# Strassen's algorithm for the first channel product of batches 4 to 7, and a new order for the second half

## The chip, the core and the metric

The kernel runs on one NeuronCore of a Trainium2 chip. Its engines work side by side, each through its own queue in order: TensorE (PE, with weight loads shown as PEld), VectorE (DVE), ScalarE (ACT), GpSimd (POOL) and SyncE (SP, which here only issues DMAs). They wait for each other by semaphores. Matmuls write to one of eight PSUM banks, and VectorE or ScalarE reads them from there. The metric is the device time of one execution in microseconds, the median of the runs.

## The reference, cut to what matters

Two layers on 8 batches of 576 tokens: an attention with random features (8 heads of 64), and a mixer over tokens and then over channels.

```python
proj = einsum('bhsd,md->bhsm', x, omega); h = proj - sum(x*x)/2
phi  = exp(h - max(h)) / sqrt(m)                   # for q and k
num  = q_p @ (k_p^T v);  den = q_p . sum(k_p);  x = num / den
h  = relu(x^T @ w_tok1) @ w_tok2;  u = x + h^T      # tokens: 576 -> 256 -> 576
h2 = relu(u @ w_ch1) @ w_ch2                        # channels: 512 -> 1536 -> 512
out = u + h2
```

The two channel products are the largest part: per batch of 512 tokens, 512 x 1536 and 1536 x 512. Inputs and output are f32; the kernel multiplies in f16 and sums in f32.

## The kernel before

A batch has 576 tokens: 512 are worked on per batch, and the 64 left of each of the eight batches are collected into one more chunk of 512, the tail chunk, whose channel mix comes last. The stages of a batch are `attention` (L521), `token_mix` (L764), and `channel_mix` (L957).

`attention`: for each pair of heads, products with omega (L656, L668), exponentials on ScalarE (L514), a maximum over features on VectorE (`km`, L680) and its reciprocal (L682), the scaling of v by it on GpSimd (`vs`, L295), the sum over tokens (L701, L708), its copy `kvsb` (L286), the numerator (L734, L736), a reciprocal (L743) and the normalisation into x (L744, or L756 on ScalarE).

`token_mix`: two products (L777, L790), a relu between, and the residual sum u on VectorE (L793). A DMA transposes u to uT (L798). `token_tail` does the same for the 64 tokens left, of two batches at a time.

`channel_mix`, first product: 12 blocks of 128 channels, each of 4 matmuls with 512 columns (L966) into a bank of its own, and a relu out of the bank on ScalarE (L290) or VectorE (L292) into `r3`. Second product (`channel_out_fast`, from batch 1 on): Strassen's algorithm in Winograd's form on halves, 7 products of 12 matmuls with 256 columns (L916) in three banks X, Y and Z, with sums S of `r3` on VectorE (L295) ahead, sums T of the weights made once (L448), and reads out of the banks into `o` (L905). Then the stores (L952, and L945 for the tail chunk).

Nothing of the order is left to a scheduler. Each step is a job with a number. The list ORDER gives the order in which all jobs are issued, and so the order in each engine's queue; SLOT gives the buffer or bank that each job takes; MOVED names the engine of jobs that don't run on their usual one. The jobs' costs and keys aren't used any more when it runs. Loads are issued from GpSimd's and SyncE's queues, stores from ScalarE's and SyncE's.

Of the kernel before, what the change touches and what calls it, by code (L numbers as in the profile page):

```python
# [9 lines left out]
FP32 = mybir.dt.float32  # L10
# [158 lines left out]
def kernel(  # L169
# [687 lines left out]
    def channel_out_fast(c, key, jr):  # L857
# [38 lines left out]
        def bank_of(b, j0):  # L896
            return (b, c, j0) if tail else (b, c)
# [173 lines left out]
```

## Time and profile before

| | |
|---|---|
| runs | 276.75, 277.55, 277.63 us; median 277.55 |
| profiled execution, first to last instruction | 275.9 us (no device time of its own is given; 1.65 us under the median) |
| granted TensorE clock | 0.996 |
| PE busy | 266.6 us, 97%, 2503 matmuls |
| DVE busy | 222.9 us, 81% |
| ACT busy | 138.1 us, 50% |
| POOL busy | 91.2 us, 33% |
| moved by DMA | 39.66 MB, mean 144 GB/s |

How to read it: busy times count an instruction from its start to its end, and overlapping instructions of one engine once. The chain of waits follows the work back from the last instruction, at each step to what released it. A group's row gives count, busy time, mean of one in ns, and the idle time of the engine in front of such instructions with what ended it.

### The profile page before, as it was taken

The page shows a single profiled execution, that of the slowest core. Times are in us where ns is not written, and L with a number is a line of the kernel's source. Part 1 is how long each engine was busy: PE and PEld are TensorE (multiplying, and loading weights), DVE is VectorE, ACT ScalarE, POOL GpSimd, SP SyncE. Part 2 cuts the span into 40 slices and gives each one's busy share as a digit, 9 for nine tenths or more (in the row PEclk, how much of TensorE's full clock was granted, in tenths as well). Part 3 has the DMA queues.
Part 4 walks back from the last instruction along what each step waited for, and adds up shares of the span by engine and source line. Part 5 has one row for each costly group of instructions (what it writes and reads, how often), then busy time and mean ns, then how long its engine had stood idle before and what let it go on. Part 6 is the DMA issues. An engine that isn't in the chain of part 4 may idle for free.

```text
span 275.9 us, 6228 instructions
## 1 busy us (share of the span) xinstructions
PE 266.6 (97%) x2503; PEld 165.5 (60%) x2503; DVE 222.9 (81%) x462; ACT 138.1 (50%) x289; POOL 91.2 (33%) x115
## 2 busy tenths in 40 slices
PE   8789999999999999999999999999999999999993
PEld 3367455444567655755676656755676477446782
DVE  3897889876998799987999899978985992675992
ACT  3999941188685338734756456636654500040200
POOL 8994492063703490075019510600043000000001
PEclk9999999999999999999999999999999999999998
DMA  7999999999998999979989994840252304021125
GB/s 195 192 209 212 190 212 177 202 193 146 203 191 133 229 176 186 151 148 171 198 184 183 232 125 123 191 90 2 97 79 77 96 0 95 2 99 53 78 83 146
DMA packets 81292, 39.66 MB, mean 144 GB/s; under 512 B 63984, under 2 KB 77040, under 8 KB 81072
## 3 DMA queue, kind: packets, MB, share of 16 engines
q0 software_dynamic: 31744, 17.74, 44.2%
q1 hardware_dynamic: 47072, 15.50, 28.7%
q10 hardware_dynamic: 2448, 6.03, 5.6%
q8 instruction: 19, 0.31, 0.5%
q14 instruction: 9, 0.07, 0.1%
HBM read 35.95 MB, written 16.52 MB: 190 GB/s over the span
## 4 chain that ended last, share of the span: by engine, by line
PE 89%; DMA 6%; POOL 3%; DVE 0%; issue 0%; POOLq 0%
PE bank L966 33%; PE bank L916 25%; PE bank L777 5%; PE bank L790 5%; DMA w1m<-in_moe_w_tok_dram 4%; PE bank L1000 4%; PE bank L734 3%; PE bank L656 3%; PE bank L668 2%; PE bank L701 2%; DMA uT<-u 2%; POOL r L319 1%; PE bank L844 1%; PE bank L816 1%; PE bank L828 1%; PE bank L736 1%
## 5 line engine op out<-in xcount | busy, mean ns | idle before, releaser
L966 PE MATMUL bank<-uT,wc 128*128 128x512 f16 x376 | 90.4, 379 | 0.3 <-DMA uT<-u 0.3
L290 ACT ACTIVATE r<-bank 128x512 f16<-128x512 f32 (+1 forms) x84 | 46.9, 597 | 77.1 <-PE bank L966 62.0
L295 POOL TENSOR_TENSOR vs<-v,vs 128x512 f16<-128x512 f16 x31 | 33.2, 1074 | 91.2 <-DVE vs L682 60.5
L966 PEld LDWEIGHTS <-wc 128*128 128x128 f16 x424 | 38.3, 98 | 37.9 <-issue 1.1
L916 PEld LDWEIGHTS <-r 128*128 128x128 f16 x384 | 36.9, 98 | 8.1 <-issue 1.2
L514 ACT ACTIVATE kp<-bank 128x512 f16<-128x512 f32 x64 | 35.6, 622 | 10.4 <-PE bank L656 10.4
L514 ACT ACTIVATE qp<-bank 128x512 f16<-128x512 f32 x64 | 36.3, 616 | 8.9 <-PE bank L668 6.0
L680 DVE TENSOR_REDUCE km<-kp 128x8 f16<-128x1024 f16 x32 | 38.6, 1206 | 2.5 <-ACT kp L514 2.4
L292 DVE TENSOR_SCALAR r<-bank 128x512 f16<-128x512 f32 (+1 forms) x42 | 27.7, 672 | 12.0 <-PE bank L966 11.2
L744 DVE TENSOR_TENSOR x<-bank,rc 128x320 f16<-128x320 f32 x62 | 30.5, 492 | 2.1
L916 PEld LDWEIGHTS <-S 128*128 128x128 f16 x288 | 27.9, 98 | 5.4 <-issue 0.3
L905 DVE TENSOR_TENSOR o<-u,bank 128x512 f32<-128x512 f16 x28 | 19.0, 679 | 6.9 <-PE bank L916 6.8
L916 PE MATMUL bank<-T,r 128*128 128x256 f16 x192 | 23.8, 273 | 0.0
L916 PE MATMUL bank<-T,S 128*128 128x256 f16 x192 | 23.6, 273 | 0.0
L916 PE MATMUL bank<-wc,r 128*128 128x256 f16 x192 | 23.6, 273 | 0.0
L945 POOL DMA_DIRECT2D out_dram<-o x2 | 1.3, 648 | 60.9 <-issue 60.9
L793 DVE TENSOR_TENSOR u<-x,bank 128x512 f16<-128x512 f16 x28 | 17.8, 681 | 1.1 <-PE bank L790 1.0
L905 DVE TENSOR_TENSOR o<-o,bank 128x512 f32<-128x512 f32 (+1 forms) x27 | 16.6, 618 | 2.2 <-PE bank L916 1.6
L734 PEld LDWEIGHTS <-qp 128*128 128x128 f16 x256 | 13.8, 98 | 7.0 <-DVE kvsb L286 0.2
L734 PE MATMUL bank<-kvsb,qp 128*128 128x65 f16 x256 | 15.6, 193 | 0.0
L743 DVE RECIPROCAL rc<-bank 128x5 f32<-128x5 f32 x62 | 11.5, 186 | 4.1 <-PE bank L736 2.7
L701 PEld LDWEIGHTS <-kp 128*128 128x128 f16 x256 | 11.5, 98 | 5.1
(120 smaller groups left out, 376.3 us busy)
## 6 DMA issues: line engine op xcount, KB each, us to landing
out_dram<-o ACTq DMA_DIRECT2D x9, 512.0 KB, 2.6
q<-in_q_dram POOLq DMA_DIRECT2D x6, 576.0 KB, 7.2
wc<-in_moe_w_ch_dram POOLq DMA_DIRECT2D x4, 768.0 KB, 10.6
k<-in_k_dram POOLq DMA_DIRECT2D x6, 512.0 KB, 6.9
v<-in_v_dram POOLq DMA_DIRECT2D x6, 512.0 KB, 8.9
out_dram<-o SPq DMA_DIRECT2D x5, 512.0 KB, 3.9
r<-in_q_dram POOLq DMA_DIRECT2D x4, 288.0 KB, 7.3
v<-in_v_dram POOLq DMA_DIRECT2D x4, 256.0 KB, 8.7
```

What stands on the lines that cost most here:

```text
L290: nc.scalar.activation(out=out, in_=in_, func=AF.Relu)
L292: nc.vector.tensor_relu(out=out, in_=in_)
L295: (nc.gpsimd if eng == "POOL" else nc.vector).tensor_tensor(**kw)
L514: nc.scalar.activation(out=out, in_=in_, func=AF.Exp, bias=0.0, scale=1.0)
L680: nc.vector.reduce_max(out=mx, in_=kpv, axis=AX.X)
L701: nc.tensor.matmul(ps[:, i, :], kpv[:, 2 * i + j // 2, j % 2, :], vs[:, i * NJ + j, 0 : D + 1], start=(i == 0 and j == 0), stop=False, ski ...
L734: nc.tensor.matmul(ps[:, k, j * 65 : (j + 1) * 65], st, s[:, i, 0 : D + 1], start=True, stop=True)
L744: nc.vector.tensor_tensor(out=t_x[place("x", b)][:, :, (2 * hp + hs[0]) * D : (2 * hp + hs[0] + n) * D].rearrange("p j (i d) -> p i j d", ...
L793: nc.vector.tensor_tensor(out=t_u[place("u", b)][:, j, :], in0=t_x[place("x", b)][:, j, :], in1=bank(n), op=ALU.add)
L905: nc.vector.tensor_tensor(out=o, in0=a, in1=ps, op=ALU.add)
L916: nc.tensor.matmul(ps[:, j * DH : (j + 1) * DH], a[:, cb, j * P : (j + 1) * P], w[:, cb, :], start=(bank_of(b, j0) not in held and j == j0 ...
L966: nc.tensor.matmul(ps, wc1[:, db, cb * P : (cb + 1) * P], moving(db), start=(db == 0), stop=(db == ND - 1))
```

## The change

The first channel product of batches 4 to 7 and of the tail chunk is made by a new function, `channel_in_fast`, in place of L966. It splits the 512 inputs, the 1536 channels and the 512 tokens in halves and forms 7 products instead of 8. For it

- four sums of uT are made per batch (512 elements per partition each), into a buffer of uT's ring, and four sums of the weights once, in two halves each (`weight_sums`), into free qT and kT buffers and a new tile `sum`;
- per pair of blocks (three in a batch) the 7 products, of 4 matmuls with 256 columns each, run through three banks. Three times the content of a bank is copied to SBUF as f32 (`keep`, on ScalarE, into r3, qp or kp buffers), and three times VectorE adds such a copy and a bank (`join`). Only one quarter of the relus still reads a bank; the others work in place in `r3`.

Besides, the steps `kt_max`, `km` and `num_out` are cut into jobs of their own (maximum, reciprocal, use), so that other work can stand between them. 12 more normalisations run on ScalarE. 12 of the sums S, one of r, 11 of the sums of uT and 5 of those of the weights run on GpSimd. The results of the tail chunk go to buffers of x's ring. r1 has 2 buffers instead of 3. Parts for other settings (HALVES and SPLIT) are empty and unused. ORDER, SLOT and MOVED are new; on TensorE the order of the first 2423 instructions is the same, up to about 118 us, and differs after it.

```diff
+    FAST_IN = 4
...
+    def weight_sums(key):
+        def quad(i, k, a):
+            return wc1[:, 2 * k + a, i * (DC // 2) : (i + 1) * (DC // 2)]
+        steps = (((1, 0), (1, 1), ALU.add), (0, (0, 0), ALU.subtract), ((0, 0), (1, 0), ALU.subtract), ((0, 1), 1, ALU.subtract))
...
+    def channel_in_fast(c, key, jt):
+        def block(k, j):
+            return (t_uT[place("uT", c)] if c < B else uTt)[:, 2 * j : 2 * j + 2, 2 * k : 2 * k + 2, :].rearrange("p j a t -> p a j t")
+        def sums():
+            return t_uT[place("uT", ("sums", c))].rearrange("p i (a j) t -> p i a j t", a=2)
+        steps = ((lambda: block(0, 1), lambda: block(0, 0)), (lambda: block(1, 1), lambda: sums()[:, 0]), (lambda: block(1, 1), lambda: block(0, 1)),
+                 (lambda: block(1, 0), lambda: sums()[:, 1]))
...
+        ops = {
+            "P1": ("X", weights(0, 0), lambda: block(0, 0), []),
+            "P2": ("Y", weights(0, 1), lambda: block(1, 0), []),
+            "P5": ("Z", sum_weights(0), lambda: sums()[:, 0], [j_sums[0][0], j_sums[1][0], j_s[0]]),
+            "P6": ("X", sum_weights(1), lambda: sums()[:, 1], [j_sums[0][1], j_sums[1][1], j_s[1]]),
+            "P7": ("X", sum_weights(2), lambda: sums()[:, 2], [j_sums[0][2], j_sums[1][2], j_s[2]]),
+            "P4": ("X", weights(1, 1), lambda: sums()[:, 3], [j_s[3]]),
+            "P3": ("Z", sum_weights(3), lambda: block(1, 1), [j_sums[0][3], j_sums[1][3]]),
+        }
...
+            def product(what, deps, m=m):
+                def go(b=b, w=w, x=x, what=what, m=m, c=c):
+                    ps, x_ = pair(b, m), x()
+                    for n in range(2):
+                        for a in range(2):
+                            nc.tensor.matmul(ps[:, n, :], w(a)[:, (2 * m + n) * P : (2 * m + n + 1) * P], x_[:, a],
+                                             start=(what in ("P1", "P2", "P5") and n == 0 and a == 0), stop=False, skip_group_check=True)
...
+            def keep(what, b, dep, m=m):
+                    copy(e_keep, kept(what, m), bank(bank_of(b, m)))
...
+            def join(what, b, i, j, deps, free, m=m):
+                    nc.vector.tensor_tensor(out=r3(i, j, m), in0=kept(what, m).rearrange("p (n t) -> p n t", n=2), in1=pair(b, m), op=ALU.add)
...
+            p1 = product("P1", [])
+            p2 = product("P2", [])
+            p5 = product("P5", [])
+            k1 = keep("P1", "X", p1)
+            c11 = join("P1", "Y", 0, 0, [k1, p2], True)
+            p6 = product("P6", [k1])
+            k2 = keep("U2", "X", p6)
+            p7 = product("P7", [k2])
+            k3 = keep("U3", "X", p7)
+            c22 = join("U3", "Z", 1, 1, [k3, p5, c11], False)
+            p3 = product("P3", [c22])
+            c12 = join("U2", "Z", 0, 1, [k2, p3], True)
+            p4 = product("P4", [k3])
...
+            def relu21(e_relu=e_relu, m=m, c=c):
+                relu_to(e_relu, r3(1, 0, m), pair("X", m))
+            def relu1(e_relu=e_relu, m=m, c=c):
+                t = t_r3[place("r3", c)][:, 2 * m : 2 * m + 2, :]
+                relu_to(e_relu, t, t)
+            def relu22(e_relu=e_relu, m=m, c=c):
+                relu_to(e_relu, r3(1, 1, m), r3(1, 1, m))
...
+        if c >= FAST_IN:
+            channel_out_fast(c, key, channel_in_fast(c, key, jt))
+            return
```

More of the change, by code (lines that the diff above doesn't have):

```diff
@@ L104 @@
+    1363: "ACT", 1364: "ACT", 1371: "POOL", 1372: "POOL", 1387: "ACT", 1388: "ACT", 1402: "DVE", 1403: "ACT",
+    1419: "ACT", 1420: "ACT", 1425: "POOL", 1427: "POOL",
 }
@@ L598, in kt_max @@
                 )
-            j_ktm = add("DVE", 1.2, kkt + 0.01, kt_max, deps=[*j_kte, j_msk], take=[("vbd", b)] if dma_in else [])
+            j_ktm = add("DVE", 0.15, kkt + 0.01, kt_mask, deps=[j_ktm, j_msk], take=take_vbd, give=[("kmt", b)])
             def vbd():
@@ new lines, in rec, with scale @@
+                def rec(hp=hp, i=hs[0], where=where):
+                    nc.vector.reciprocal(out=t_rc[place("rc", (b, hp, i))], in_=where()[:, 0, 0 : 5 * 65].rearrange("p (j d) -> p j d", d=65)[:, :, D])
+                j_r = add("DVE", 0.1, kno, rec, deps=[j_n], take=[("rc", (b, hp, hs[0]))])
+                e_num = engine("DVE")
+                def scale(hp=hp, i=hs[0], where=where, e_num=e_num):
+                    to = t_x[place("x", b)][:, :, (2 * hp + i) * D : (2 * hp + i + 1) * D]
+                    ps = where()[:, 0, 0 : 5 * 65].rearrange("p (j d) -> p j d", d=65)[:, :, 0:D]
+                    rc = t_rc[place("rc", (b, hp, i))]
+                    if e_num == "ACT":
+                        for j in range(NJ + 1):
+                            nc.scalar.activation(out=to[:, j], in_=ps[:, j], func=AF.Copy, scale=rc[:, j : j + 1])
+                    else:
+                        nc.vector.tensor_tensor(out=to, in0=ps, in1=rc.unsqueeze(2).broadcast_to((P, NJ + 1, D)), op=ALU.mult)
@@ L762, in attention @@
+                last_x.append(add(e_num, 0.45, kno, scale, deps=[j_r], take=[("x", b)], give=[at, ("rc", (b, hp, hs[0]))]))
         return last_x
@@ L865, in channel_out_fast @@
             part = slice(g * NH // 2, (g + 1) * NH // 2)
-            need = [jr[cb + NH * e] for cb in range(part.start, part.stop) for e in range(2)]
+            need = [x for cb in range(part.start, part.stop) for e in range(2) for x in jr[cb + NH * e]]
             steps = (
@@ L872, in channel_out_fast @@
             )
-            prev = []
+            done = []
             for k, (i, what, op) in enumerate(steps):
@@ L897, in bank_of, with o_tag, o_of, go @@
             return (b, c, j0) if tail else (b, c)
+        def o_tag(i):
+            return ("x", ("o", i)) if tail else ("o", (c, i))
+        def o_of(i):
+            if tail:
+                return t_x[place(*o_tag(i))].rearrange("p j d -> p (j d)")[:, 0 : 4 * DM].bitcast(FP32).rearrange("p (j d) -> p j d", j=2)
+            return t_o[place(*o_tag(i))]
         def read(k, b, i, e, base, deps, free, j0=0, j1=2):
-            def go(c=c):
-                o = t_o[place("o", (c, i))][:, j0:j1, DH * e : DH * e + DH]
+            e_read = engine("DVE")
+            def go(c=c, e_read=e_read):
+                o = o_of(i)[:, j0:j1, DH * e : DH * e + DH]
                 ps = bank(bank_of(b, j0)).rearrange("p (j d) -> p j d", j=2)[:, j0:j1]
+                if e_read == "ACT":
+                    nc.scalar.copy(out=o, in_=ps)
+                    return
                 u = t_u[place("u", c)] if c < B else t_ut
@@ L944, in store @@
                         to = out[4 * i : 4 * i + 4, SM:S, cols].rearrange("(j h) t d -> h t j d", h=2)[h]
-                        (nc.scalar if eng == "ACT" else nc.sync if eng == "SP" else nc.gpsimd).dma_start(out=to[:, js], in_=t_o[place("o", (c, i))][half[h], js, cols])
-                    dma(eng, key + 0.9, 0.3, store, deps=[outs[need, j] for j in range(*js)], give=[("o", (c, i))],
+                        (nc.scalar if eng == "ACT" else nc.sync if eng == "SP" else nc.gpsimd).dma_start(out=to[:, js], in_=o_of(i)[half[h], js, cols])
+                    dma(eng, key + 0.9, 0.3, store, deps=[outs[need, j] for j in range(*js)], give=[o_tag(i)],
                         cost=0.412 if js[1] - js[0] == 1 else 0.414)
@@ L951, in store @@
             def store(i=i, eng=eng):
-                (nc.scalar if eng == "ACT" else nc.sync).dma_start(out=out[c, 0:SM, :].rearrange("(p j) d -> p j d", j=NJ)[:, 2 * i : 2 * i + 2, :], in_=t_o[place("o", (c, i))])
-            dma(eng, key + 0.9 + 0.1 * i, 1.3, store, deps=[outs[x, 0] for x in need], give=[("o", (c, i))], cost=0.4)
+                (nc.scalar if eng == "ACT" else nc.sync).dma_start(out=out[c, 0:SM, :].rearrange("(p j) d -> p j d", j=NJ)[:, 2 * i : 2 * i + 2, :], in_=o_of(i))
@@ new lines, in channel_out_fast, with sum_of, go @@
+            dma(eng, key + 0.9 + 0.1 * i, 1.3, store, deps=[outs[x, 0] for x in need], give=[o_tag(i)], cost=0.4)
+    j_sums = []
+    def sum_of(i, k):
+        n = 2 * i + k
+        if n < 6:
+            tag = "qT" if n < 3 else "kT"
+            return (t_qT if n < 3 else t_kT)[place(tag, "sums")][:, n % 3 * (DC // 2) : n % 3 * (DC // 2) + DC // 2]
+        return t_sum[:, n - 6]
+    def weight_sums(key):
[3 more added lines that the diff above has]
+        for a in range(2):
+            done = []
+            for i, (x, y, op) in enumerate(steps):
+                e_sum = engine("DVE")
+                def go(i=i, a=a, x=x, y=y, op=op, e_sum=e_sum):
+                    x, y = [sum_of(z, a) if isinstance(z, int) else quad(*z, a) for z in (x, y)]
+                    tt(e_sum, out=sum_of(i, a), in0=x, in1=y, op=op)
+                need = [done[z] for z in (x, y) if isinstance(z, int)]
+                n = 2 * i + a
+                done.append(add(e_sum, 0.46, key, go, deps=[*need, *j_wc1], take=[("qT" if n < 3 else "kT", "sums")] if n < 6 else []))
+            j_sums.append(done)
@@ L984, in relu @@
                 relu_to(e_relu, t_r3[place("r3", c)][:, cb, :], bank(n))
-            jr[cb] = (add(e_relu, 0.5, key + 0.5 * pos / NCB, relu, deps=[j1], take=[("r3", c)], give=[("bank", n)]))
+            jr[cb] = [add(e_relu, 0.5, key + 0.5 * pos / NCB, relu, deps=[j1], take=[("r3", c)], give=[("bank", n)])]
         if fast:
@@ L1001, in channel_mix @@
                 prev = add("PE", mm(4, 512) + (mm(4, P) if part == 2 else 0.0), key + 0.5 + 0.5 * (3 * j + part) / 12, c2,
-                           deps=[prev, *jr[4 * part : 4 * part + 4], *j_wc2], take=[("bank", n)], give=[("r3", c), ("uT", c)])
+                           deps=[prev, *(x for done in jr[4 * part : 4 * part + 4] for x in done), *j_wc2], take=[("bank", n)], give=[("r3", c), ("uT", c)])
             k2 = key + 0.5 + 0.5 * (3 * j + 3) / 12
```

186 lines of the change are left out of this document (127 added, 59 removed), and 131 rows, old and new, of the table ORDER.

## The prediction

> **What bounds the kernel now.** I read the page first, then the chain of work that ended last, then busy times by stage, then groups and timelines. Two rows of the busy list and the engine shares of the chain, from the page:
> ```profile
> PE 266.6 (97%) x2503; PEld 165.5 (60%) x2503; DVE 222.9 (81%) x462; ACT 138.1 (50%) x289; POOL 91.2 (33%) x115
> PE 89%; DMA 6%; POOL 3%; DVE 0%; issue 0%; POOLq 0%
> ```
> TensorE (PE) is busy for 97% of the span and 89% of the chain lies on it. VectorE (DVE) has 81%. Pieces of that chain in order of time (start, us, what):
> ```profile
> 224.50 5.24 PE bank L916 x48
> 234.09 13.81 PE bank L966 x64
> 260.94 10.51 PE bank L916 x96
> 271.48 0.42 DVE o L905
> ```
> They give the prices of a matmul where TensorE runs back to back: 13.81/64 = 0.2158 us for 512 columns (L966, first channel product) and 5.24/48 = 0.1092 us for 256 columns (L916, second channel product, already by Strassen's algorithm). The last piece is one VectorE read; after it 4.0 us of stores end the span at 275.9. The second half by stage (a stage ends where VectorE ends a batch's residual sum, batches 4 to 7; the last row is the rest up to the end of TensorE; columns PE, PEld, DVE, ACT, POOL busy, then clock and DMA):
> ```profile
> 111.50:141.70 30.20, 30.20 (x306) 19.80 (x304) 26.67 (x57) 16.72 (x35) 9.58 (x11) 1.00 0.98 168
> 141.70:168.90 27.20, 27.20 (x257) 16.86 (x256) 24.82 (x53) 14.70 (x30) 12.19 (x14) 1.00 0.98 169
> 168.90:198.00 29.10, 29.10 (x284) 18.42 (x282) 25.43 (x52) 16.85 (x34) 4.86 (x5) 1.00 0.44 101
> 198.00:227.90 29.90, 29.90 (x275) 19.55 (x270) 25.25 (x53) 12.56 (x25) 5.20 (x5) 1.00 0.29 63
> 227.90:271.50 43.60, 43.54 (x305) 29.58 (x303) 28.90 (x56) 5.92 (x11) 1.29 (x2) 1.00 0.23 72
> sum 160.00, PE 159.94 PEld 104.22 DVE 131.07 ACT 66.75 POOL 33.13; mean PE 31.99 PEld 20.84 DVE 26.21 ACT 13.35 POOL 6.63
> ```
> TensorE never stands still in these 160 us at full clock (1.00). So matmul time taken away is gained, as long as nothing else becomes late. VectorE is the next: 131.1 of 160, idle 3.5, 2.4, 3.7 and 4.7 us in the four stages and 14.7 in the last.
>
> **The change, part by part.** The instruction orders of the two kernels are the same on TensorE, bank numbers apart, until about 118 us; whatever happens happens in the second half.
>
> *TensorE.* For batches 4 to 7 and the tail chunk, 48 matmuls of 512 columns become 84 of 256 (7 products instead of 8 on quarter blocks). 240 x 0.2158 = 51.8 goes, 420 x 0.1092 = 45.9 comes: -5.9 us. Each new matmul has a weight load of its own, as those of L916 have, and 0.1092 was measured with them. By stage, from the instruction orders: between the residual sums of batches 4 and 5, 84 of 256 and 64 of 512 columns become 144 and 16 (60 x 0.1092 - 48 x 0.2158 = -3.8). The five stages change by +3.4, -3.8, -4.6, +0.3 and -1.1, since work has also moved between them, and take TensorE about 33, 24, 24.5, 28 and 46 us.
>
> [...]
>
> *VectorE, ScalarE, GpSimd.* The groups used (out<-in, count | busy, mean ns | idle before):
> ```profile
> L292 DVE TENSOR_SCALAR r<-bank 128x512 f16<-128x512 f32 x40 | 26.9, 684 | 11.7 <-PE bank L966 11.2
> L744 DVE TENSOR_TENSOR x<-bank,rc 128x320 f16<-128x320 f32 x62 | 30.5, 492 | 2.1
> L295 DVE TENSOR_TENSOR S<-r 128x768 f16<-128x768 f16 x16 | 8.8, 553 | 1.4 <-ACT r L290 1.3
> L905 DVE TENSOR_TENSOR o<-o,bank 128x512 f32<-128x512 f32 x21 | 14.1, 674 | 1.6 <-PE bank L916 1.1 <-issue 0.2
> L680 DVE TENSOR_REDUCE km<-kp 128x8 f16<-128x1024 f16 x32 | 38.6, 1206 | 2.5 <-ACT kp L514 2.4
> L545 DVE COPY ktt<-kT 128x256 f16<-128x256 f16 x1 | 0.2, 227 | 0.0
> L286 DVE CAST kvsb<-bank 128x130 f16<-128x130 f32 x12 | 3.4, 287 | 5.1 <-PE bank L708 5.1
> L290 ACT ACTIVATE r<-bank 128x512 f16<-128x512 f32 x82 | 46.1, 602 | 76.6 <-PE bank L966 62.0 <-PE bank L777 8.9 <-DVE o L905 5.4
> L756 ACT ACTIVATE x<-bank,rc 128x64 f16<-128x64 f32 x10 | 2.3, 340 | 0.0
> L295 POOL TENSOR_TENSOR vs<-v,vs 128x512 f16<-128x512 f16 x31 | 33.2, 1074 | 91.2 <-DVE vs L682 60.5 <-PE bank L668 22.3 <-PE bank L966 4.5
> L295 POOL TENSOR_TENSOR T<-vt,T 128x1024 f16<-128x1024 f16 x1 | 1.9, 1941 | 0.0
> ```
> VectorE loses 15 relus out of PSUM (15 x 0.684 = 10.3), 13 sums S and r that GpSimd takes (7.2), and 12 normalisations that ScalarE takes (5.9): -23.4. It gains 45 joins, a kept f32 product plus a bank, priced as the read o<-o,bank (45 x 0.674 = 30.3); 9 sums of the product's input, 512 elements; 3 weight sums (1.7); 3 copies kvsb (0.9); 7 relus of 1024 and 6 of 512 elements inside SBUF. An input sum lies between 0.23 (the copy) and 0.55 (768 elements); I take 0.40, near the row of its own kind: 3.6. No row shows a relu from SBUF to SBUF. Bounds: 0.23 below; above, one from PSUM, 0.684 for 512, twice that for 1024. I take 0.30 and 0.45, nearer to the SBUF rows: 4.9. Sum +41.4, net +18.0.
>
> These are durations, and VectorE overlaps them. From its timeline:
> ```profile
> 128.24 0.18 DVE L743 RECIPROCAL rc<-bank 128x5 f32<-128x5 f32 x1
> 128.45 0.49 DVE L744 TENSOR_TENSOR x<-bank,rc 128x320 f16<-128x320 f32 x1
> 128.86 0.68 DVE L292 TENSOR_SCALAR r<-bank 128x512 f16<-128x512 f32 x1
> ```
> An independent successor starts 0.08 us before the end (128.86 against 128.94), a dependent one 0.03 after it (128.45 against 128.42). So 33 more instructions are worth 33 x 0.08 = -2.6; and the change splits reciprocals from their users, so that other work lies between them: some ten pairs in each of the first four stages, 0.11 each, -4.4. Net +11.0: 131.1 becomes 142. By stage, from the counts in the instruction orders and these prices: 30.8, 24.2, 21.5, 25.5, 39.9. Stage two is the tight one: 9 joins (6.1), 2 input sums (0.8) and 4 SBUF relus (1.65) come; 4 relus (2.7), 2 reads (1.35), 3 normalisations (1.5) and 4 sums (2.2) go; 24.2 us of VectorE stand against 24.4 of TensorE, where 2.4 were idle before.
>
> ScalarE: relus from PSUM fall by 40 (24.1) and ten come back; 45 copies of a bank, 17 SBUF relus and 60 scalings of 64 columns (20.4) come. With 0.60 for a copy and 1.04 for 1024 elements (twice the 602 row, less a start) that is +42, 67 becoming 109 of some 155: off the path, unless one copy is late for the product that waits for its bank (three in a row per pair of blocks). That wait is new on VectorE too: a join waits for ScalarE's copy, and behind it in VectorE's queue stand the normalisations and kvsb copies that the next batch's attention on TensorE needs; its price is in the stall below. GpSimd: 17 sums of 768 elements, between 1.07 and 1.94, at 1.5; one sum of r, 1.5; 11 of 512, 1.07: about +38, 33 becoming 71. Loads on GpSimd's queue stay in number but stand behind these sums; they are issued a batch ahead and I cost that at nothing. The tail's results go to x buffers, at nothing: all batches are done with them by then.
>
> *What is late next.* The residual sum is transposed by a DMA before the next first product. The DMA's times to land (from the tile's view), a residual sum, and the first product on its result:
> ```profile
> DMA to landing us min/median/max: 4.3/5.4/6.0
> 166.39 2.47 DVE L793 TENSOR_TENSOR u<-x,bank 128x512 f16<-128x512 f16 x4
> 176.21 1.03 PE L966 MATMUL bank<-uT,wc 128*128 128x512 f16 x4
> ```
> Before, the sum ended at 168.86 and the product began 7.35 us later, so 1.3 to 3 us were spare. In the new order of TensorE, the work between batch 5's last token product and its first channel product adds up to 6.7 us; the sum, 0.9 after the token product, and 5.4 to 6.0 leave 0.4 or nothing. A microsecond that VectorE is late in stage two is a microsecond of TensorE.
>
> So the stall lies between 0 (VectorE packs as its new idle of 1.9, 0.2, 3.0 and 2.8 allows) and, if the idle of before is forced and stays, 1.6 + 2.2 + 0.7 + 1.9 = 6.4. No row says which; I take half, 3.2. In the last stage VectorE has 6 us free, and I take nothing there. The sum: 275.9 - 5.9 + 3.2 = 273.2 of span. The profiled execution's span is 1.65 below the median of the runs (277.55), and I take the same around it after: 274.9 us.
>
> **Does GpSimd block VectorE?** One place in the trace has both read two SBUF tensors at once:
> ```profile
> 14.52 1.02 DVE L295 TENSOR_TENSOR vs<-v,vs 128x512 f16<-128x512 f16 x1
> 14.96 1.50 POOL L295 TENSOR_TENSOR vs<-v,vs 128x512 f16<-128x512 f16 x1
> ```
> GpSimd's sum took 1.50 instead of 1.07: 0.43 longer, to about where VectorE's ended plus its own length. In the changed kernel 29 more sums on GpSimd meet VectorE's SBUF sums; a meeting costs 0.43 or more to whoever comes second. [...] I price this as a rival: six meetings that VectorE loses, 6 x 0.43 = 2.6, on top of the 3.2.
>
> **Rivals.**
> - *All of it arrives*: no stall, 277.55 - 5.9 = 271.6. For it: TensorE stood still for 0.06 us in 160 with VectorE at 82%. Against: stage two leaves VectorE 0.2.
> - *No change*: the meetings with GpSimd, or all of the old idle: 277.55 - 5.9 + 5.8 to 6.4 = 277.5 to 278.1.
> - *Slower, VectorE becomes the bound*: SBUF relus run like those from PSUM. 7 x (1.37 - 0.45) + 6 x (0.684 - 0.30) = 8.7 more, of which 5.8 in the four stages; with the 3.2 the stall is 9, 280.7. It decides once stalls pass 5.9. For it: VectorE at 142 of 156 has little room. Against: the SBUF rows (768 elements in 0.553, the copy in 0.227) are all faster per element than PSUM's.
> [...]
>
> **How the numbers follow.** Chances: forecast 0.47 (its own range 272.8 to 276.7), all arrives 0.17, no change 0.12, VectorE the bound 0.23, the rule 0.01. About 0.3% (0.8 us) is what this kernel's runs can tell from no change. Faster is 0.47 and 0.17, less 0.01 of the forecast's upper edge: 0.63; same 0.13; slower 0.24. The range 271.4 to 280.2 leaves out the upper half of the VectorE case and a little below.
>
> **What would show it.** Right: after 118 us, matmuls of 256 columns at 0.109; VectorE 140 to 146 busy after 111 us; TensorE idle of 2 to 4 us, in front of the first channel product (DMA uT<-u) and of products that wait for a VectorE join. Wrong: SBUF relus far from 0.30 and 0.45; joins longer than 0.68; VectorE's or GpSimd's sums stretched beyond 0.55 and 1.5; TensorE waiting in the last stage on ScalarE's copies.

## The result, and the profile after

| | before | changed |
|---|---|---|
| runs, median | 277.25 us (276.75 to 277.63) | 284.92 us (284.45 to 287.25) |
| ratio, 95% interval | | 1.030 (1.027 to 1.033) |
| profiled execution: time, span | 277.55, 275.9 us | 284.45, 282.7 us |

The change made the kernel 3% slower; 274.9 us and the range up to 280.2 were both missed. (Ratios leave out disturbed executions, so a ratio further down can differ from the quotient of the medians, most of all for the run `e9_four`, where five of ten are left out.)

The page of the changed kernel, busy list and engine shares of the chain that ended last:
```profile
PE 264.1 (93%) x2683; PEld 183.6 (65%) x2683; DVE 242.0 (86%) x495; ACT 170.5 (60%) x378; POOL 133.4 (47%) x144
PE 65%; DVE 15%; DMA 9%; issue 5%; POOL 4%; DVEq 0%; POOLq 0%
```
TensorE has fallen from 97% of the span to 93%, and only 65% of the chain lies on it where it was 89%. The second half by the same stages as in the prediction (each ends with a batch's residual sum, the last with TensorE's end; columns PE, PEld, DVE, ACT, POOL busy):
```profile
112.86:146.82 33.96, 32.66 (x333) 21.32 (x330) 31.90 (x65) 21.75 (x53) 21.26 (x20) 1.00 0.95 153
146.82:175.22 28.40, 26.22 (x292) 19.68 (x288) 27.85 (x55) 21.15 (x52) 19.06 (x19) 1.00 0.83 139
175.22:203.09 27.87, 24.92 (x283) 19.08 (x280) 22.61 (x50) 20.22 (x50) 13.52 (x12) 1.00 0.52 106
203.09:232.92 29.83, 28.14 (x290) 22.32 (x290) 25.79 (x55) 18.86 (x44) 14.17 (x11) 1.00 0.34 85
232.92:277.73 44.81, 44.51 (x405) 39.25 (x402) 40.81 (x79) 17.09 (x28) 7.19 (x6) 1.00 0.21 66
sum 164.87, PE 156.44 PEld 121.65 DVE 148.96 ACT 99.06 POOL 75.20; mean PE 31.29 PEld 24.33 DVE 29.79 ACT 19.81 POOL 15.04
```
TensorE's work fell as it should, if by less: 159.94 became 156.44. But it now stands still for 8.4 us of 164.87, where it stood still for 0.06 in 160. VectorE was to come to 142 us and has 148.96; in the second stage it is busy for 27.85 of 28.40 us. What TensorE waits for in the second half, from the view of waits (us in total, times, longest; three more waits have 0.7 together, and none is for GpSimd):
```profile
PE bank L1076 <- DMA uT<-u: 4.3, 2, 2.7
PE bank L771 <- DVE kvsb L309: 1.3, 1, 1.3
PE bank L964 <- DVE o L944: 1.1, 1, 1.1
PE bank L771 <- DVE r L1100: 1.0, 1, 1.0
```
Without any stall the span would have been 275.9 - 5.9 = 270.0. It is 282.7, so 12.7 us have to be found: the 8.4 in which TensorE stands still, 2.4 of its busy time that did not go away (156.44 instead of 154.0), 0.5 behind its end, and 1.4 where I had expected nothing. Batch 3's residual sum ends at 112.86 instead of 111.48, before any matmul has changed.

Three places in the timelines suggest causes. First, eight normalisations near 70 us. Before:
```profile
70.24 0.18 DVE L743 RECIPROCAL rc<-bank 128x5 f32<-128x5 f32 x1
70.46 0.49 DVE L744 TENSOR_TENSOR x<-bank,rc 128x320 f16<-128x320 f32 x1
70.87 0.18 DVE L743 RECIPROCAL rc<-bank 128x5 f32<-128x5 f32 x1
```
After:
```profile
70.51 0.19 DVE L778 RECIPROCAL rc<-bank 128x5 f32<-128x5 f32 x1
70.74 0.49 DVE L789 TENSOR_TENSOR x<-bank,rc 128x320 f16<-128x320 f32 x1
71.33 0.20 DVE L778 RECIPROCAL rc<-bank 128x5 f32<-128x5 f32 x1
```
A pair took 0.63 us (70.24 to 70.87) and takes 0.82 (70.51 to 71.33). The next reciprocal used to start 0.08 before the normalisation ended; now it starts 0.10 after. Both do the same work. The new kernel has a ring of eight small buffers `rc`, but its list of buffers gives all eight pairs the same one, so a reciprocal must wait until the normalisation before it has read that buffer.

Second, VectorE and GpSimd in stage two, in the timeline after:
```profile
154.42 1.19 DVE L715 TENSOR_REDUCE km<-kp 128x8 f16<-128x1024 f16 x1
155.53 2.64 DVE L619 TENSOR_TENSOR vbd<-kmt,mask 128x8 f16<-128x8 f16 x1
166.60 0.75 DVE L315 TENSOR_SCALAR r<-r 128x1024 f16<-128x1024 f16 x2
167.35 1.89 DVE L318 TENSOR_TENSOR S<-r 128x768 f16<-128x768 f16 x2
...
154.88 0.94 POOL L360 DMA_DIRECT2D v<-in_v_dram  x1
155.84 1.17 POOL L318 TENSOR_TENSOR uT<-uT 128x512 f16<-128x512 f16 x1
156.95 1.16 POOL L318 TENSOR_TENSOR uT<-uT,uT 128x512 f16<-128x512 f16 x1
167.69 1.13 POOL L318 TENSOR_TENSOR vs<-v,vs 128x512 f16<-128x512 f16 x1 [6.32 <-DMA v<-in_v_dram]
```
The product of 8 elements by a mask, 0.18 us elsewhere, took 2.64: it ended when GpSimd's second sum did. It had begun 0.3 us before the first of them, while GpSimd was still issuing a load. Of the two S sums at 167.35, 1.89 us together, the second took 1.41 where 0.55 is usual; it began after GpSimd's. In all, seven VectorE instructions are 7.9 us longer than their kind (0.27, 1.33, 2.45, 0.86, 0.86, 0.72, 1.41), each with both inputs in SBUF. Before, one was, by 0.27, in the timeline of that kernel:
```profile
118.46 1.06 POOL L295 TENSOR_TENSOR vs<-v,vs 128x512 f16<-128x512 f16 x1 [0.34 <-DVE vs L682]
119.10 0.46 DVE L593 TENSOR_TENSOR vbd<-rct,mask 128x8 f16<-128x8 f16 x1
```
In the changed kernel VectorE's busy time without them would be 141.

Third, the DMA uT<-u of batch 5, in the view of DMA issues from 174 to 184 us:
```profile
out_dram<-o ACTq DMA_DIRECT2D x1, 512.0 KB, 3.0
uT<-u SPq DMA_TRANSPOSE x1, 7.2
```
It landed 7.2 us after its issue; before, the longest was 6.0, and that of batch 5 took 4.8. A store of 512 KB was issued at 174.98, the DMA at 175.25.

### The profile page after: what moved, and what is told of

Read it like the earlier page. It is cut to its first block, busy times and chain, and to the rows that moved or that the text cites. A ratio compares the mean times of both kernels' runs of the same rounds, so it can differ in the third digit from the quotient of the medians.

```text
span 282.7 us, 6782 instructions
## 1 busy us (share of the span) xinstructions
PE 264.1 (93%) x2683; PEld 183.6 (65%) x2683; DVE 242.0 (86%) x495; ACT 170.5 (60%) x378; POOL 133.4 (47%) x144
## 3 DMA queue, kind: packets, MB, share of 16 engines
q1 hardware_dynamic: 46928, 15.37, 27.6%
## 4 chain that ended last, share of the span: by engine, by line
PE 65%; DVE 15%; DMA 9%; issue 5%; POOL 4%; DVEq 0%; POOLq 0%
PE bank L964 20%; PE bank L1147 12%; PE bank L1076 12%; DMA uT<-u 5%; DMA w1m<-in_moe_w_tok_dram 4%; PE bank L806 3%; PE bank L819 3%; DVE x L789 3%; PE bank L1181 2%; DVE r L1100 2%; PE bank L682 2%; PE bank L694 2%; PE bank L738 2%; PE bank L771 2%; DVE rc L778 1%
## 5 line engine op out<-in xcount | busy, mean ns | idle before, releaser
L313 ACT ACTIVATE r<-bank 128x512 f16<-128x512 f32 (+1 forms) x54 | 31.0, 600 | 24.5 <-PE bank L1147 14.3
L1147 PE MATMUL bank<-uT,wc 128*128 128x512 f16 x184 | 44.4, 379 | 0.2 <-DVE x L789 0.2
L537 ACT ACTIVATE kp<-bank 128x512 f16<-128x512 f32 x64 | 36.4, 624 | 9.5 <-PE bank L682 9.4
L537 ACT ACTIVATE qp<-bank 128x512 f16<-128x512 f32 x64 | 37.1, 621 | 6.1 <-PE bank L694 6.0
L1147 PEld LDWEIGHTS <-wc 128*128 128x128 f16 x184 | 16.5, 98 | 16.6 <-issue 1.4
L1076 PE MATMUL bank<-uT,wc 128*128 128x256 f16 x156 | 21.4, 273 | 4.3 <-DMA uT<-u 4.3
L789 DVE TENSOR_TENSOR x<-bank,rc 128x320 f16<-128x320 f32 x50 | 24.1, 486 | 1.2
L318 POOL TENSOR_TENSOR S<-r 128x768 f16<-128x768 f16 x4 | 6.6, 1640 | 37.9 <-PE bank L964 21.6
L1076 PEld LDWEIGHTS <-wc 128*128 128x128 f16 x180 | 17.0, 98 | 7.2 <-DMA uT<-u 4.9
L315 DVE TENSOR_SCALAR r<-bank 128x512 f16<-128x512 f32 (+1 forms) x27 | 17.6, 659 | 3.4 <-PE bank L1147 2.6
L787 ACT ACTIVATE x<-bank,rc 128x64 f16<-128x64 f32 x70 | 15.9, 337 | 6.4 <-DVE rc L778 6.4
```

The costliest lines, as they stand in the source:

```text
L313: nc.scalar.activation(out=out, in_=in_, func=AF.Relu)
L315: nc.vector.tensor_relu(out=out, in_=in_)
L318: (nc.gpsimd if eng == "POOL" else nc.vector).tensor_tensor(**kw)
L537: nc.scalar.activation(out=out, in_=in_, func=AF.Exp, bias=0.0, scale=1.0)
L789: nc.vector.tensor_tensor(out=to, in0=ps, in1=rc.unsqueeze(2).broadcast_to((P, NJ + 1, D)), op=ALU.mult)
L1076: nc.tensor.matmul(ps[:, n, :], w(a)[:, (2 * m + n) * P : (2 * m + n + 1) * P], x_[:, a], start=(what in ("P1", "P2", "P5") and n == 0 and ...
```

## The experiments

Times of stages from the residual sums, as in the windows above (first: up to batch 3's sum; rest: from TensorE's end to the span's), each from one profiled execution. A star marks 3.4 us in which TensorE's granted clock was 0.5. In stage three of the changed kernel it makes 1.6 us (27.87 without it, 29.47 with it); the last section comes back to this.

| kernel | first | 1 | 2 | 3 | 4 | 5 | rest | median us | ratio to before (95%) |
|---|---|---|---|---|---|---|---|---|---|
| before | 111.48 | 30.2 | 27.2 | 29.1 | 29.9 | 43.6 | 4.4 | 277.25 | |
| changed | 112.86 | 33.96 | 28.40 | 27.87 | 29.83 | 44.81 | 4.9 | 284.92 | 1.030 (1.027-1.033) |
| after_again | 113.24 | 33.94 | 28.40 | 29.47* | 29.85 | 44.81 | 5.0 | 284.57 | 1.025 (1.021-1.029) |
| e1_rc | 111.05 | 33.93 | 29.50 | 29.33* | 29.84 | 44.81 | 4.9 | 286.22 | 1.033 (1.026-1.039) |
| e2_nosums | 114.07 | 32.67 | 24.77 | 29.31* | 28.74 | 44.31 | 5.0 | 281.29 | 1.013 (1.008-1.017) |
| e3_last | 113.07 | 33.95 | 28.41 | 29.43* | 29.82 | 45.23 | 5.3 | 286.74 | 1.034 (1.031-1.037) |
| e4_mask | 113.14 | 35.30 | 28.57 | 28.55* | 28.77 | 44.81 | 4.9 | 286.49 | 1.037 (1.030-1.044) |
| e5_store | 114.51* | 33.95 | 28.40 | 27.17 | 28.22 | 44.81 | 5.1 | 283.95 | 1.025 (1.021-1.030) |
| e6_dve | 112.77 | 35.76 | 28.60* | 31.13* | 35.28** | 45.20 | 5.0 | 295.02 | 1.061 (1.055-1.067) |
| e7_three | 112.10 | 32.56 | 24.87 | 26.22 | 28.92 | 44.18 | 5.7 | 276.33 | 0.997 (0.995-0.999) |
| e8_recip | 112.85 | 34.28 | 29.62* | 29.21* | 28.93 | 44.81 | 5.0 | 285.43 | 1.030 (1.026-1.034) |
| e9_four | 119.01*** | 34.05 | 28.87 | 26.18 | 28.96 | 44.81 | 4.9 | 278.93 | 0.997 (0.993-1.001) |
| e10_five | 110.94 | 34.06 | 28.59* | 26.16 | 28.97 | 44.81 | 4.9 | 280.01 | 1.005 (1.000-1.010) |
| e11_seven | 111.40 | 32.82 | 25.06 | 26.18 | 28.76 | 44.82 | 5.5 | 275.59 | 0.993 (0.991-0.995) |

Where nothing is edited and no star stands, each of the stages 1 to 5 comes out the same to 0.05 us, so they can be compared singly. The first stretch varies more (112.77 to 113.24 where nothing in it is edited). The profile of `e9_four` is that of its longest execution, of 288.54 us.

### The rc waits alone: `e1_rc`

```diff
-                    i = self.held[tag, name] = int(next(slots))
+                    i = int(next(slots))
+                    if tag == "rc":
+                        i = next(x % 8 for x in range(self.turn, self.turn + 8) if not left.get(owner.get((tag, x % 8))))
+                        self.turn = i + 1
+                    self.held[tag, name] = i
```


> The eight rc buffers are taken in turn instead of as listed. Theory A (the loss has two named parts: waits of a reciprocal for the normalisation that still reads its rc buffer, 0.2 us each, and VectorE's sums of two SBUF tensors that stand still while GpSimd works, 7.9 us in seven instructions): each pair of reciprocal and normalisation in the run of eight near 70 us falls from 0.82 to 0.62 us, batch 3's residual sum ends at 111.4 to 111.7 instead of 112.9, the time falls by 1.2 to 2.0 us, to 283 to 283.7. Theory B (VectorE's added work is what bounds the second half, the first half's 1.4 us come from elsewhere): the pairs get shorter but the time stays at 284.9 within 0.5.

The pairs near 70 us, in the timeline of this run, are back to 0.63 us (70.25 to 70.88), and the sum of batch 3 ends at 111.05:
```profile
70.25 0.18 DVE L783 RECIPROCAL rc<-bank 128x5 f32<-128x5 f32 x1
70.47 0.49 DVE L794 TENSOR_TENSOR x<-bank,rc 128x320 f16<-128x320 f32 x1
70.88 0.18 DVE L783 RECIPROCAL rc<-bank 128x5 f32<-128x5 f32 x1
```
So the first half's loss is the rc waits: the stretch up to there is 1.8 us shorter. The time did not fall. With everything 1.8 us earlier, other instructions met, and stage two grew by 1.1. VectorE's input sum uT<-uT,uT took 2.94 us instead of 0.43:
```profile
150.26 2.94 DVE L323 TENSOR_TENSOR uT<-uT,uT 128x512 f16<-128x512 f16 x1
...
151.24 1.66 POOL L323 TENSOR_TENSOR S<-r,S 128x768 f16<-128x768 f16 x1
```
Theory A's part in the first half holds; its sum over the kernel doesn't, since the stretches are not a fixed amount. This run also shows what no run before did, two relus between SBUF tensors beside a GpSimd sum:
```profile
165.95 1.62 DVE L320 TENSOR_SCALAR r<-r 128x1024 f16<-128x1024 f16 x2
...
166.24 1.05 POOL L323 TENSOR_TENSOR vs<-v,vs 128x512 f16<-128x512 f16 x1 [6.91 <-DMA v<-in_v_dram]
```
Two of them took 0.75 in the changed kernel (at 166.60, above) and 1.62 here: the second ended at 167.57, 0.3 us after GpSimd's vs<-v,vs.

### GpSimd's sums left out: `e2_nosums`

```diff
                 def go(what=what, op=op, part=part, e_sum=e_sum, c=c, g=g, k=k):
+                    if e_sum == "POOL":
+                        return
                     o, a, b = what()
```
The same two lines stand in the sums of the weights and of the product's input (29 sums in all; a memset of one buffer in the first half replaces what the products would read uninitialised).

> The 28 sums that the change gives to GpSimd are left out on both engines (16 or 17 of weights and relus, 11 of the product's input); TensorE's products read what the buffers held before. VectorE's work stays as it is. Theory A: the stretched instructions (the mask product of 2.64 us among them) return to 0.2 and 0.55 us, VectorE's busy time falls from 242 to 234 to 236, the time by 5 to 8 us, to 277 to 280. Theory B: VectorE's stretches lay beside slack, the time falls by less than 2 us, 283 to 285.

Stages one to three of this run:
```profile
114.07:146.74 32.67, 32.67 (x335) 21.40 (x332) 30.53 (x65) 21.75 (x53) 14.39 (x16) 1.00 1.05 159
146.74:171.51 24.77, 24.77 (x286) 19.46 (x282) 23.95 (x54) 20.83 (x51) 10.35 (x12) 1.00 0.94 159
171.51:200.81 29.30, 26.74 (x283) 19.94 (x283) 22.70 (x49) 20.02 (x49) 3.81 (x4) 0.94 0.51 101
```
VectorE does what it did and is down from 31.90 and 27.85 to 30.53 and 23.95; TensorE no longer stands still in the first two stages, which are 1.3 and 3.6 us shorter. Theory B falls: the stretches did not lie beside slack, and VectorE's own added work, at this amount, is not what held TensorE up. In this run GpSimd's loads alone stretched nothing either: they are all still there, and of VectorE's instructions only two mask products are longer than their kind, 0.46 and 0.58 us. But 2.56 us of idle remain in stage three, before batch 5's first product, and the time stays above the forecast of 277 to 280.

### Sums of the last stage back on VectorE: `e3_last`

```diff
-    1363: "ACT", 1364: "ACT", 1371: "POOL", 1372: "POOL", 1387: "ACT", ...
-    1419: "ACT", 1420: "ACT", 1425: "POOL", 1427: "POOL",
+    1363: "ACT", 1364: "ACT", 1387: "ACT", ...
+    1419: "ACT", 1420: "ACT",
```


> The tail chunk's four GpSimd sums (two of S, two of the product's input) go back to VectorE. Theory A: no sum meets GpSimd in the last stage, the 1.96 us S sum at 267 falls to 0.55 and two sums of 1.64 become 0.55: the last stage gets 2.0 to 3.6 us shorter, 281.3 to 282.9. Theory B: VectorE takes 1.9 us more and the time stays or grows by up to 1 us, 284.9 to 286.

The last stage went from 44.81 to 45.23, as theory B said. The stretch of 1.41 was gone and nothing gained: with all four sums on VectorE TensorE needed as long as with the two engines and their meeting. Theory A was wrong for this stage, and a stretch there is no loss by itself.

### The mask product on GpSimd: `e4_mask`

```diff
+        for n, ahead in [(662, 663), (846, 847), (1024, 1025), (1200, 1201)]:
+            order.remove(n)
+            order.insert(order.index(ahead), n)
...
+            e_mask = "POOL" if len(plan.jobs) in (662, 846, 1024, 1200) else "DVE"
```


> The small mask product (vbd<-kmt,mask, 8 elements) of batches 4 to 7 runs on GpSimd, right ahead of its vbd product, instead of on VectorE. Theory A: the 2.64 and 0.92 us that it took on VectorE in stages two and three are gone and take TensorE's wait behind them along: 2 to 3 us less, 282 to 283. Theory B: the next instruction of VectorE with two SBUF inputs, or the DMA uT<-u behind it, takes the wait over: less than 1 us, 284 to 285.

Theory B came true. VectorE's next instruction of the kind, an input sum, waited in stage two in the mask product's place, in the timeline of this run:
```profile
153.57 2.96 DVE L326 TENSOR_TENSOR uT<-uT,uT 128x512 f16<-128x512 f16 x1
...
154.59 1.66 POOL L326 TENSOR_TENSOR S<-r,S 128x768 f16<-128x768 f16 x1
```
and two S sums met GpSimd in stage one, which grew by 1.3. To take one instruction out of the way moved the meeting.

### The stores, and the changed kernel again: `e5_store`, `after_again`

```diff
+        for n, ahead in [(647, 922)]:
+            order.remove(n)
+            order.insert(order.index(ahead), n)
...
-    831: "ACT",
```


> The changed kernel once more, as it is, so that the three others can be compared with it on the same chip: 284 to 287 us; TensorE idle in the second half for 8 to 9 us in the profile, 2.7 and 1.6 of them before the first products of batches 5 and 6, and the reciprocal pairs near 70 us 0.82 us apart.

> Two stores are moved away from the transposing DMAs uT<-u: that of batch 3's first half goes 50 places up in the order (its data is there 14 us before it is issued), that of batch 4's first half goes to SP's queue, behind the DMA. Theory C (three causes: GpSimd's sums, the rc waits, and stores of 512 KB that run beside the DMA uT<-u): from the residual sum to the first product of batches 5 and 6 it is 5.0 to 5.8 us instead of 7.2 and 6.5, TensorE's idle time there falls from 4.3 to 1 to 2 us, the time falls by 2.2 to 3.5 us against the changed kernel on this chip. Theory D (these waits follow from VectorE's late sums, whatever the DMA does): less than 0.8 us.

In stages three and four, compared with the changed kernel's 27.87 and 29.83, this run has 27.17 and 28.22: 2.3 us less, as theory C said, and TensorE's idle time there falls from 4.3 to 2.0. From the sum to the next product it is 6.5 and 4.9 us (7.2 and 6.5 before the edit), so batch 5's missed the 5.0 to 5.8. Its DMA still takes 6.5 us to land; the store beside it made 0.7 of the 7.2, and what makes the rest above the 4.8 of the kernel before was not tried. The median moved by only 0.6 us and the fastest run by 0.3 (283.88 to 283.55), and the intervals overlap. The stages of one profile each carry the verdict here; the times don't confirm it.

### All sums on VectorE: `e6_dve`

The 29 entries "POOL" of these sums are taken out of MOVED.

> All 29 sums that the change gives to GpSimd run on VectorE: 18 of 768 elements at 0.55 and 11 of 512 at 0.42, 14.5 us of work more, and no sum of it that meets GpSimd beyond those of the attention. If the stretches (7.9 us in seven instructions) are worth as much as VectorE's own time: VectorE's busy time 248 to 250, the time 3 to 6 us above the changed kernel. If the stretches cost more than their length, since TensorE waits behind them: 0 to 3 us below it. If they cost nothing: 10 us or more above.

The page's busy list and the longest wait of this run:
```profile
PE 272.6 (93%) x2683; PEld 187.3 (64%) x2683; DVE 248.4 (85%) x524; ACT 170.7 (58%) x378; POOL 91.2 (31%) x115
...
PE bank L964 <- DVE S L318: 5.0, 2, 4.3
```
VectorE's busy time came out as expected, 248.4, the time 10 us above the changed kernel. By the letter that is the last outcome, that the stretches cost nothing. But TensorE waits up to 4.3 us for one S sum that stands behind other work in VectorE's queue, and its clock was at half for 13.6 us. At 1.6 us for each 3.4 that is an estimated 6.4 of the 10 us, and what is left would fit the first outcome; so this run does not decide between them. In this order the sums are better on GpSimd, even with their meetings.

### Three causes together: `e7_three`

The edits of `e1_rc`, `e2_nosums` and `e5_store` in one kernel, so again without the 29 sums.

> Three things together: the 29 GpSimd sums left out as in the second run, rc buffers in turn, and the two stores moved. Theory C: these are the causes, so TensorE's idle time in the second half is below 1.5 us, the time 272 to 275, 3 to 5 us below the kernel before. If something else of the change holds TensorE up (the joins that wait for ScalarE's copies, VectorE's order): 277 or more, and the idle time names it.

TensorE's idle time in the second half fell from 8.4 to 1.8 us, and the span from 282.7 to 274.6: the three account for 8.1 of the 12.7 us, though leaving out the sums takes away GpSimd's work as well as the meetings. The time, 276.3, missed the 272 to 275. What remains against 270.0 is 1.8 of idle (all of it before batches 5 and 6, on the DMA uT<-u), 0.9 in TensorE's own work (154.94 against 159.94 - 5.9), 1.3 behind TensorE's end, where the last stores finish, and 0.6 in the first half.

### The mask product without a second input: `e8_recip`

```diff
             def kt_mask():
+                if b >= 4:
+                    with nc.allow_low_precision(reason="fp16 operand of the matmul"):
+                        for i in range(2):
+                            nc.vector.reciprocal(out=vbd_of(b)[half[i], :, i, D], in_=t_kmt[place("kmt", b)][half[i], 0])
+                    return
```
The reciprocal ahead of it falls away.

> The mask product of batches 4 to 7 (vbd<-kmt,mask, two SBUF tensors) and the reciprocal ahead of it become two reciprocals of 64 partitions that write into vbd directly; reciprocals did not get longer beside GpSimd's sums in the trace (0.21 against 0.21). Nothing else changes. If the second input makes VectorE wait (theory C): the 2.64 and 0.92 us become 2 x 0.17, stage two gets 1.5 to 2.5 and stage three 0.4 to 0.8 us shorter, the time falls by 2 to 3 us to 281.5 to 282.7. If the next sum or relu between SBUF tensors takes the wait over, as the 2.96 us uT sum did when the product moved to GpSimd: less than 1 us.

The reciprocals took their 0.2 us beside GpSimd's sums. But the second outcome came: uT<-uT,uT met GpSimd again and took 3.17 us, and the time stayed. In stage three (27.6 without its star) and four it brought 0.3 and 0.9.

### Four and five edits: `e9_four`, `e10_five`

`e9_four` has the rc ring, the stores and the reciprocals; `e10_five` also moves one vbd product, job 1025, ahead of job 922 in the order.

> Reciprocals instead of the mask product, rc buffers in turn, and the two stores moved, all sums still on GpSimd. Added up from the stages of the single runs: 1.5 to 1.8 from the rc buffers, 2.3 from the stores, 2 to 3 from the mask product, from 284.6: 277.5 to 278.8, no difference from the kernel before. If the meetings of VectorE and GpSimd only move to other instructions when the work shifts: 280 to 283.

> As the run before it, and GpSimd's vbd product of batch 6 stands ahead of its vs product in the order, where GpSimd idled, so that it ends before VectorE's sums of S near 168. If that meeting cost its length: 0.8 us less than the run before it. If the wait of the S sums lay beside other work: the same.

`e9_four` measured 278.93 us, its ten runs lie between 276.2 and 288.5, and the ratio is 0.997 (0.993 to 1.001): no difference from the kernel before, as the adding up said. `e10_five` measured 280.01, ratio 1.005. The S sums near 168 no longer met the vbd product; what that is worth in stage two can only be estimated, since it has a star (28.59, some 27.0 without it, against 28.87), and the time shows nothing of it. In both, qT<-wc and uT<-uT,uT still took 1.87 and 2.94 to 2.96 us.

### Two of GpSimd's sums in another place: `e11_seven`

```diff
-        for n, ahead in [(647, 922), (1025, 922)]:
+        for n, ahead in [(647, 922), (1025, 922), (755, 751), (628, 876)]:
```


> As the run before it (reciprocals for the mask product, rc in turn, two stores and batch 6's vbd product moved), and two of GpSimd's sums change place in its queue: the first weight sum kT<-wc goes behind qT<-qT,wc, which waits for VectorE's two sums qT<-wc itself, and batch 3's last S sum goes ahead of a vs product and four loads, away from VectorE's input sums of batch 4. If a ready GpSimd sum is what VectorE's sums stood still for (theory C): qT<-wc falls from 1.87 to 0.52 to 0.55 us and uT<-uT,uT from 2.94 to 0.42, stage one gets 0.8 to 1.1 and stage two 1.6 to 2.6 us shorter, the time goes to 273.5 to 275.5, ratio to the kernel before 0.985 to 0.993. If the meetings only move again, or TensorE waits for the sums and the vs product that now come later: 276 to 279.

All of the change's products, joins and sums are done, on the same engines as in the changed kernel; the stretches fell from 7.9 us to 2.0 (0.63 and 1.41). The timeline near the weight sums, the page's busy list, its chain, and the stages:
```profile
125.72 0.98 DVE L331 TENSOR_TENSOR qT<-wc 128x768 f16<-128x768 f16 x2
149.88 0.43 DVE L331 TENSOR_TENSOR uT<-uT,uT 128x512 f16<-128x512 f16 x1
```
```profile
PE 263.3 (96%) x2683; PEld 183.8 (67%) x2683; DVE 235.4 (86%) x495; ACT 169.7 (62%) x378; POOL 132.4 (48%) x144
PE 75%; DVE 6%; DMA 6%; ACT 5%; POOL 4%; issue 2%; SPq 0%; POOLq 0%; DVEq 0%
```
```profile
111.40:144.22 32.82, 32.82 (x340) 21.59 (x337) 30.55 (x65) 21.76 (x53) 21.18 (x20) 1.00 1.02 159
144.22:169.28 25.06, 24.81 (x278) 19.33 (x278) 24.55 (x56) 20.93 (x51) 18.52 (x19) 1.00 1.02 178
169.28:195.47 26.19, 24.93 (x281) 19.02 (x281) 22.23 (x50) 19.96 (x49) 13.02 (x11) 1.00 0.52 93
195.47:224.23 28.76, 28.38 (x300) 22.46 (x294) 25.80 (x54) 19.05 (x44) 14.67 (x12) 1.00 0.37 88
224.23:269.05 44.82, 44.52 (x405) 39.24 (x402) 40.84 (x80) 17.09 (x28) 6.84 (x6) 1.00 0.20 66
```
Against the run before it, stage one is 1.2 us shorter, and stage two 3.5, of which some 1.6 were that run's star; against the changed kernel it is 1.1 and 3.3. Theory C holds, though the time is 0.1 above its range. At 275.59 us this version is 3.3% below the changed kernel and 0.7% (0.5 to 0.9%) below the one before. GpSimd has its 132 us of work as before: what its sums cost TensorE lay not in their amount but in where they stood. Of the 9 us between the changed kernel and this one the places of the two sums are one part (the ratio went from 1.005 to 0.993 by them alone); rc buffers, stores, reciprocals and the vbd product are the others.

## Why the prediction was wrong, point by point

- *TensorE, -5.9 us.* The direction held, the size not in full: -3.5 in the changed kernel (159.94 to 156.44), -5.0 in `e7_three`, where it hardly waits. Where the missing part sits is not shown. The page's price of a matmul was the right one to take: in the changed kernel's chain 108 of the new matmuls in a row, from 243.45, took 11.79 us, 0.1092 each. No run shows anything for the chance of 0.01 given to a rule: TensorE's work fell.
- *VectorE, 131 to 142 us.* The prices held: joins 0.67 to 0.68, input sums 0.42 (0.40), SBUF relus 0.42 and 0.285 (0.45 and 0.30). Less the stretches VectorE comes to 141 in the changed kernel, and to 142 in `e11_seven` (143.97 less 2.0). So *VectorE becomes the bound* was wrong in its mechanism, slow relus, though its 280.7 lies nearest to the 284.92. VectorE is the bound of stage two, but through waiting.
- *Split reciprocals, -4.4, and "whatever happens happens in the second half".* Wrong in sign where pairs stand alone. I had read the instruction order, not which rc buffer each pair takes; with one buffer in a row each pair became 0.2 longer. 1.4 us, shown by `e1_rc`. For the second half the -4.4 is not shown by itself.
- *GpSimd blocks VectorE, six meetings at 0.43 = 2.6.* This is the step that failed: a term of the stall that was left out of the forecast and mis-sized in its rival. The mechanism was named and its size taken from the one row at 14.52, where GpSimd came second. That row was not the only meeting in the trace before. Near 119 us, in the lines shown above, VectorE came second, and its mask product took 0.46 us instead of 0.19. In the changed kernel VectorE stood still for 7.9 us in seven meetings, or 1.1 each, once through two of GpSimd's instructions. In five of them it began second, and waited for as much as GpSimd had left; the two longest, 3.8 us together, began while GpSimd still issued loads ahead of its sum. Leaving the sums out gave back 4.9 us in stages one and two, where TensorE then did not wait (`e2_nosums`). I kept the term out of the forecast and in a rival of chance 0.12, since nothing told me how often the two would meet; with GpSimd's work in stages one and two going from 21.8 to 40.3 us, it should have carried the range.
- *The stall, half of 0 to 6.4.* The upper end was not a bound: it counted VectorE's old idle time and left out VectorE's stretched time. TensorE stood still for 8.4 us.
- *The DMA uT<-u, 4.3 to 6.0, slack 0.4 or nothing.* The slack was read rightly, and TensorE's longest waits, 4.3 of its 8.4 us, stand there. The duration was wrong: 7.2, and still 6.5 without the store beside it. I had not looked at which stores the new order puts beside the DMA. By the stages of `e5_store` the two stores are worth 2.3 us; what else makes batch 5's DMA long stays open.
- *The last stage, nothing.* The 28 and 46 us given for the last two stages don't follow from their changes of +0.3 and -1.1, which give 30.2 and 42.5. Together the two took 74.6 instead of 72.7, and 73.6 in `e11_seven`. TensorE's work in them is what was forecast (28.14 + 44.51 = 72.65), only split otherwise: the last stage now has 402 matmuls of 256 columns, 43.9 us at the page's price. The 1.9 on top are waiting: 1.7 in stage four, nearly all of it for the DMA uT<-u of batch 6, and 0.3 in the last. So a stall of nothing was nearly right for the last stage, and `e3_last` agrees that the stretch of 1.41 is not a loss there.

## What to carry to other kernels

Where two engines get in each other's way, as VectorE and GpSimd do here, their meetings belong into the sum with the length of the whole instruction that is in the way (in the changed kernel seven meetings cost 7.9 us, the longest 2.45), and the order of both queues has to be read side by side; total busy time says nothing on it (GpSimd was busy for 133.4 us in the changed kernel, where VectorE's stretches made 7.9 us, and for 132.4 in `e11_seven`, where they made 2.0). Here a meeting was removed by moving GpSimd's ready work to where VectorE had none of that kind, while taking one VectorE instruction away passed the wait on to the next (`e4_mask`, `e8_recip`). When an edit gives an operation a ring of buffers, see which buffer is really taken, and when it moves a DMA on the critical path, see what else is on the DMA engines then (batch 5's uT<-u took 7.2 us beside a store and 6.5 without it).

## What the runs showed of the hardware

In the changed kernel VectorE stood still beside a GpSimd instruction on SBUF when both of its inputs were in SBUF (mask product 2.64 instead of 0.18, S sum 1.41 instead of 0.55), and in `e1_rc` also in a relu from SBUF to SBUF (1.62 for two instead of 0.75). It did not in maxima, in reciprocals and in sums of SBUF with PSUM. In the changed kernel 13 maxima km that began in a GpSimd sum, at least 0.3 us ahead of its end, took 1.207 us and the 19 others 1.213; 19 reciprocals rc that began in one took 0.184 and the 45 others 0.186; 8 reads o<-o,bank 0.674 and the 13 others 0.672. A single VectorE instruction also lost to several of GpSimd's in a row: uT<-uT ended at 157.01, uT<-uT,uT at 158.11, and the mask product, begun ahead of both at 155.53, at 158.17. VectorE also stood still where GpSimd was, by the trace, only issuing loads with a ready sum behind them. In the changed kernel the first of two sums qT<-wc took 1.88 us, while the kT<-wc sum behind the loads began at 129.20:
```profile
127.19 2.35 DVE L318 TENSOR_TENSOR qT<-wc 128x768 f16<-128x768 f16 x2
```
The input sum of 2.94 us in `e1_rc` and the mask product of 2.64 began like that too, 1.0 and 0.3 us ahead of GpSimd's sum. In `e11_seven`, where that place in the queue has a sum that isn't ready, the two sums qT<-wc took 0.98, and in `e2_nosums`, with the loads and no sum behind them, 0.99. Why a sum that has not begun should matter is open.

In these runs a wait of TensorE could cost more than its length. In the second profile of the changed kernel, `after_again`, batch 5's wait and what follows (columns as above, granted clock third from the end):
```profile
180.00:183.40 3.40, 0.81 (x12) 0.63 (x11) 0.86 (x3) 0.60 (x3) 0.55 (x1) 1.00 1.13 147
183.40:186.80 3.40, 3.40 (x21) 2.38 (x18) 3.02 (x6) 1.62 (x6) 3.32 (x4) 0.50 0.41 88
```
After a wait of 2.6 us TensorE had 21 matmuls in 3.4 us at half clock. Of the 11 waits of 2.1 to 2.7 us in the profiled runs (the before and changed kernels and all experiments), 9 were followed by such a stretch within 2.5 us of their end (the stars of stage two in `e8_recip` and `e10_five` and all those of stage three), of those between 1.0 and 2.0 us none; the two waits of 4.3 us (stage four of `e6_dve`, the first stretch of `e9_four`) each had 6.8 us at half clock. Once, in `e6_dve` near 149 us, it came after short waits alone, and twice near 11 us. The changed kernel's own wait of 2.7 us before batch 5's first product had none (clock 1.00 in stage three), so 2.1 to 2.7 us of waiting were mostly enough, not always. The half clock may be a reason why the times of the changed kernel, with such a wait, spread by 2.8 us, and those of `e11_seven`, without one, by 1.2; but those of `e3_last`, with one, spread by 1.2 too. So in this kernel a stall of over 2 us on TensorE is to be priced at some 1.6 us more than its length, an estimate from stage three of the changed kernel and the 9 of 11.
